# The small operations of the denominators on GpSimd, and attention a step farther behind the numerators

## The chip, the core and the metric

The kernel runs on one core of one Trainium2 chip. The metric is the device time of one execution in microseconds (us); lower is better. The core's engines run side by side, each works through its own queue of instructions in order, and they wait for one another by semaphores: TensorE (PE in the profile, with its weight loads as PEld), VectorE (DVE), ScalarE (ACT), GpSimd (POOL) and SyncE (SP), which here only issues DMA transfers.

## The reference

Everything is float32. With 2048 positions of 512 numbers, 32 heads of 16 numbers and a hidden size of 1792, it computes

```
g = sigmoid((x * gate_w).sum(-1))                      # one gate per position
q, k, v = split(x @ wqkv)                              # 32 heads x 16
phi(y)  = [softmax(y @ w_phi), softmax(-(y @ w_phi))]  # 32 features per head
kv      = sum over positions of phi(k)^T v             # per head 32 x 16
z       = sum over positions of phi(k)                 # per head 32
o       = (phi(q) @ kv) / (phi(q) . z + 1e-6)          # numerator / denominator
a       = o @ wo
b       = relu(x @ w1 + b1)^2 @ w2 + b2
out     = g * a + (1 - g) * b
```

## The kernel before

Float32 products are made from two rounded halves, a high one (h) and a low one (l), and three passes: high times high, low times high, high times low (`mm3`). A tile name that ends in h or l is such a half. The halves of a tile are made by a copy on ScalarE and a subtraction on VectorE or GpSimd (`split`).

The first 273 us make the hidden layer of the dense branch, the features of the keys with the sums kv and z, and the queries. None of that is touched by the change, and nothing more is said of it. The rest is a second stage of 56 **steps**, 14 for each of four blocks of 512 positions. A step multiplies one 128-wide slice of the hidden layer by one slice of w2 (`down`): four groups, for the 128-row parts of the block, into the four PSUM banks uA, uE, uB0 and uB1, three matmuls of 512 columns each. The hidden slices come back from HBM into tiles O0h/O0l (even steps) and O1h/O1l (odd steps), some as finished halves, some through a tile named ring that is split on the way. A slice is loaded or split up to four steps before its step.

Between the steps stand, for each block i:

- `do_e(i, k)`, for the four quarters k of the heads: load the queries, the exponentials, their sums sm and the reciprocals r = 1/sm.
- `do_phi(i, k)`: the denominators, and the features of the queries scaled by them. GpSimd multiplies the exponentials by z into ez (two halves of 128x512; there is one ez tile, so the next quarter waits until it is read); VectorE sums ez into dz (128x64); then come the **small operations**: dz times r; den, the sum of the two softmax parts of dz plus 1e-6; its reciprocal; and w = r times the reciprocal. VectorE scales the exponentials by w (128x1024) and transposes them (128x1024) into a tile that TensorE reads. For block 0 these tiles are the four named XA, for the other blocks the halves of tb (quarters 0 and 1) and phiT (quarters 2 and 3).
- `do_n(i)`: the **numerators**, one burst of 32 small matmuls (32x32 by 512) into the four PSUM banks vB, vE, kv, vA. It takes the quarters in the order 0, 2, 1, 3; quarter 3 is its last fourth. Then `split` reads the four banks into XS10h to XS21l.
- `attend(i, c)`, for c = 0 to 3: 12 matmuls of the numerators with wo into one of the same four banks, and one operation on VectorE that adds the result, times the gate, to the output row.
- `evict` at the end of a block's 14 steps: ScalarE copies a bank of `down` into XA times 1-g, and a **row addition** (128x512) adds that to the output row, on VectorE or GpSimd.

**What sets the order.** Nothing is issued as the code runs through. Each call of an engine is recorded in a plan. `Plan.order` (line 238) then goes through the plan with costs per instruction (`lengths`), due times counted back from TensorE's work, and one lock for VectorE and GpSimd operations with two wide inputs (`op.two`), and it writes one queue per engine. What is recorded on `nc.either` goes to VectorE or GpSimd, whichever the plan would start first. TensorE's groups keep the recorded order, but the plan may bring forward a group out of the first five (`LOOK`) if the groups ahead of it are not ready in its reckoning. On the chip every queue is in order, and an instruction whose input is late holds up what stands behind it.

The steps at which bursts and attention are recorded come from a table and a loop near the end (`steps`):

```
NUM = [13, 26, 38, 50]
when(NUM[i], do_n, i)
for c in range(NC):
    when(NUM[i] + 2 + c, attend, i, c)
```

Of the kernel before, what the change touches and what calls it, by code (L numbers as in the profile page):

```python
# [11 lines left out]
ALU = mybir.AluOpType  # L12
# [5 lines left out]
P = 128  # L18
S, D, H, DH, F = 2048, 512, 32, 16, 1792
# [16 lines left out]
CALM, LATE = 16.0, 2.0  # L36
PARTED = 8
FOLD = 8
NUM = [13, 26, 38, 50]
AT = [0, 1, 2, 4, 8, 11, 14, 17, 20, 23, 26, 29, 32, 35, 38, 41]  # L40


# [333 lines left out]
def tile_gated_mix(ctx: ExitStack, tc: tile.TileContext, xT, xn, wqT, wkT, wphi, wv, wo, w1, b1, w2, b2, gw, out):  # L376
    nc = Plan(tc.nc)
# [7 lines left out]
    def buf(tag, n=512, bufs=1, dtype=F32):  # L385

        i = turns[tag] = turns.get(tag, -1) + 1
        return View(Buffer(sbuf, shadows[n], f"{tag}_{i % bufs}", n, dtype), shadows[n])
# [298 lines left out]
    def scaled(e3, w):  # L687
        nc.vector.tensor_tensor(e3, e3, w.unsqueeze(2).to_broadcast([P, 2 * H, DH]), ALU.mult)
        return e3.rearrange("p h f -> p (h f)")
# [114 lines left out]
    def do_phi(i, k):  # L804
        e3, r = st["e", i, k]
        ez = buf("ez", 2 * D)
        by_rows = lambda t: t.rearrange("p (n f) -> p n f", f=4 * DH)
        e = by_rows(e3.rearrange("p h f -> p (h f)"))
        for half in range(2):
            s = slice(half * NG, (half + 1) * NG)  # L810
            z = zb[:, k * 4 * DH:(k + 1) * 4 * DH].unsqueeze(1).to_broadcast([P, NG, 4 * DH])
            nc.gpsimd.tensor_tensor(by_rows(ez)[:, s, :], e[:, s, :], z, ALU.mult)
        dz, w = small("dz", 2 * H, 2), small("w", 2 * H, 1)
        nc.vector.tensor_reduce(dz, ez.rearrange("p (h f) -> p h f", f=DH), AX.X, ALU.add)
        nc.either.tensor_tensor(dz, dz, r, ALU.mult)
        pair = lambda t: t.rearrange("p (h t) -> p h t", t=2)
        den = pair(dz)[:, :, 0]
        nc.vector.scalar_tensor_tensor(den, den, 1e-6, pair(dz)[:, :, 1], ALU.add, ALU.add)
        nc.vector.reciprocal(den, den)
        nc.either.tensor_tensor(pair(w), pair(r), den.unsqueeze(2).to_broadcast([P, H, 2]), ALU.mult)  # L820
        phi = scaled(e3, w)
        if i == 0:
            pt = buf(E_PLACES[k], 2 * D)
        else:
            if k % 2 == 0:
                st["pt"] = buf(("tb", "phiT")[k // 2], 4 * D)
            pt = st["pt"][:, k % 2 * 2 * D:(k % 2 + 1) * 2 * D]
        st["pt", i, k] = pt
        nc.vector.transpose(pt, phi)
# [173 lines left out]
    when = lambda s, f, *a: steps.setdefault(s, []).append(lambda: f(*a))  # L1003
# [3 lines left out]
    for i in range(NB):  # L1007
        when(AT[4 * i], gates, ORDER_B[i])
        for k in range(NK):
            if i:  # L1010
                when(max(AT[4 * i + k], NUM[0] if i == 1 else 0), do_e, i, k)
            when(max(AT[4 * i + k] + 2, NUM[i - 1] if i else 0), do_phi, i, k)
        when(NUM[i], do_n, i)
        for c in range(NC):
            when(NUM[i] + 2 + c, attend, i, c)
    for t in range(NT):
        for f in steps.get(t, ()):
            f()
        i, f = divmod(t, NF)
# [80 lines left out]
```

## Time and profile before

| | us |
|---|---|
| three runs | 484.23, 484.39, 485.07 (median 484.39) |
| the profiled execution, its time | 484.48 |
| its span, first to last instruction | 482.7 |
| TensorE busy | 477.8 (99%) |
| VectorE busy | 398.2 (82%) |
| ScalarE busy | 247.5 (51%) |
| GpSimd busy | 188.0 (39%) |

A row of a group gives engine, operation, output <- inputs, partitions x elements, the count, the busy time in us and the mean ns of one. A row of the timeline gives the start in us from the start of the span, the duration in us, the engine, the operation, and in brackets the idle time before it with what ended it. All of the work has source line 363, a helper that issues the plan, so tiles tell the rows apart. Tile names in the order of a queue carry the number of the operation that made them; the profile leaves these numbers out.

### The profile page before, as it was taken

What the parts mean: (1) busy time and instruction counts of PE and PEld (TensorE: products, weight loads), DVE (VectorE), ACT (ScalarE), POOL (GpSimd) and SP (SyncE); (2) the same over time, 40 slices, a digit from 0 to 9 for tenths busy, and PEclk for the clock granted to TensorE, in tenths of its full rate; (3) what the DMA queues carried; (4) which work ended last, traced back from release to release, by engine and by line L of the source; (5) the groups of instructions that cost most, each with busy time, mean ns of one, the idle gap of its engine ahead of it and who ended that gap; (6) DMA issues with size and microseconds to landing.
All of it is one profiled execution on the core that took longest, in us unless ns stands there. A gap on an engine that the chain in (4) does not pass through costs nothing.

```text
span 482.7 us, 9482 instructions
## 1 busy us (share of the span) xinstructions
PE 477.8 (99%) x3513; PEld 383.7 (79%) x3513; DVE 398.2 (82%) x565; ACT 247.5 (51%) x440; POOL 188.0 (39%) x160
## 2 busy tenths in 40 slices
PE   9999999999999999999999999999999999999997
PEld 4877788888888888888888888778878887888786
DVE  3997799988898757999888838999999999896214
ACT  5897879642698666426688803442245304420400
POOL 1010545743563202121022328667577808950000
PEclk9999999999999999999999999999999999999999
DMA  7999876885587779954799887824632572225302
GB/s 272 380 396 325 285 270 252 262 309 185 178 281 252 264 265 317 292 197 165 240 335 353 304 293 271 270 96 172 221 109 67 162 252 88 65 89 209 119 0 87
DMA packets 61654, 107.98 MB, mean 224 GB/s; under 512 B 6952, under 2 KB 11432, under 8 KB 61608
## 3 DMA queue, kind: packets, MB, share of 16 engines
q1 hardware_dynamic: 60768, 106.33, 64.0%
q10 hardware_dynamic: 808, 1.05, 0.9%
q8 instruction: 27, 0.44, 0.4%
q14 instruction: 19, 0.16, 0.1%
q0 software_dynamic: 32, 0.01, 0.0%
HBM read 62.27 MB, written 45.09 MB: 222 GB/s over the span
## 4 chain that ended last, share of the span: by engine, by line
PE 98%; DVE 1%; issue 0%
PE uB L363 30%; PE uA L363 18%; PE uE L363 17%; PE vB L363 11%; PE vE L363 8%; PE vA L363 8%; PE kv L363 5%; DVE tb L363 0%; DVE vE L363 0%; DVE uE L363 0%; DVE KT10l L363 0%; DVE KT10h L363 0%; DVE XS40l L363 0%; DVE XS30l L363 0%; DVE KT31l L363 0%; DVE O1l L363 0%
## 5 line engine op out<-in xcount | busy, mean ns | idle before, releaser
L363 POOL TENSOR_TENSOR ez<-XA,vext 128x512 f32<-128x512 f32 x24 | 34.9, 1469 | 13.7 <-ACT XA L363 6.5
L363 PE MATMUL uA<-XA,O0h 128*128 128x512 f32 x128 | 39.7, 391 | 0.0
L363 ACT ACTIVATE XA<-XA 128x512 f32<-128x512 f32 x24 | 13.9, 627 | 40.3 <-DVE XA L363 40.3
L363 ACT ACTIVATE row<-row 128x512 f32<-128x512 f32 x56 | 34.0, 623 | 0.3
L363 POOL TENSOR_TENSOR row<-row,wo 128x512 fp32r<-128x512 f32 x8 | 10.4, 1299 | 50.3 <-ACT wo L363 40.6
L363 PEld LDWEIGHTS uA<-XA,O0h 128*128 128x128 f32 x128 | 23.9, 188 | 5.1 <-ACT row L363 0.2
L363 PE MATMUL uA<-XA,O0l 128*128 128x512 f32 x64 | 24.9, 389 | 0.0
L363 POOL TENSOR_TENSOR row<-row,b2b 128x512 fp32r<-128x512 f32 x9 | 13.0, 1449 | 23.6 <-ACT b2b L363 16.3
L363 ACT ACTIVATE O0h<-ring 128x512 fp32r<-128x512 f32 x17 | 10.7, 628 | 21.0 <-PE uB L363 10.1
L363 DVE TENSOR_REDUCE dz<-ez 128x64 f32<-128x1024 f32 x16 | 19.3, 1209 | 1.8 <-POOL ez L363 1.2
L363 PE MATMUL uB<-XA,O3h 128*128 128x512 f32 x64 | 19.8, 391 | 0.0
L363 POOL TENSOR_TENSOR row<-row,XA 128x512 f32<-128x512 f32 x12 | 18.5, 1556 | 2.3 <-ACT row L363 1.3
L363 DVE SCALAR_TENSOR_TENSOR xn<-xn,gwb 128x512 f32<-128x512 f32 x16 | 11.3, 709 | 7.8 <-DMA xn<-in_xn 7.8
L363 DVE RECIPROCAL r<-sm 128x64 f32<-128x64 f32 x32 | 17.2, 539 | 0.3
L363 ACT ACTIVATE O1h<-ring 128x512 fp32r<-128x512 f32 x17 | 10.7, 627 | 13.0 <-PE uB L363 12.5
L363 DVE TENSOR_TENSOR XA<-XA,w 128x1024 f32<-128x1024 f32 x12 | 17.0, 1414 | 0.0
L363 ACT ACTIVATE wo<-row 128x512 fp32r<-128x512 f32 x17 | 10.7, 627 | 12.3 <-DMA hkept<-wo 10.2
L363 DVE TENSOR_REDUCE sm<-e 128x64 f32<-128x1024 f32 x11 | 13.4, 1216 | 3.6 <-ACT e L363 3.5
L363 ACT ACTIVATE row<-b2b,rest 128x512 f32<-128x512 f32 x16 | 10.8, 715 | 9.5 <-DMA out<-row 5.9
L363 POOL TENSOR_TENSOR O0l<-ring,O0h 128x512 fp32r<-128x512 f32 x9 | 14.2, 1582 | 3.5 <-ACT O0h L363 2.6
L363 DVE TENSOR_TENSOR e<-e,r 128x1024 f32<-128x1024 f32 x11 | 15.1, 1370 | 0.2
L363 POOL TENSOR_TENSOR O1l<-ring,O1h 128x512 fp32r<-128x512 f32 x9 | 13.1, 1460 | 5.3 <-ACT O1h L363 5.3
(936 smaller groups left out, 1742.4 us busy)
## 6 DMA issues: line engine op xcount, KB each, us to landing
hkept<-row SPq DMA_DIRECT2D x56, 256.0 KB, 4.2
ring<-hkept SPq DMA_DIRECT2D x24, 256.0 KB, 2.7
hkept<-b2b SPq DMA_DIRECT2D x16, 256.0 KB, 3.2
hkept<-wo SPq DMA_DIRECT2D x16, 256.0 KB, 4.1
xn<-in_xn SPq DMA_DIRECT2D x16, 256.0 KB, 4.8
O0h<-hkept SPq DMA_DIRECT2D x16, 256.0 KB, 3.2
O0l<-hkept SPq DMA_DIRECT2D x16, 256.0 KB, 3.4
O1h<-hkept SPq DMA_DIRECT2D x16, 256.0 KB, 3.7
```

Of the source, the lines that this page charges most:

```text
L363: call(*map(real, op.args), **{k: real(a) for k, a in op.kw.items()})
```

## The change

Three of the small operations are now bound to GpSimd. The operation on VectorE that added the two parts and 1e-6 in one instruction is two: the addition on GpSimd, and the addition of the constant on VectorE. The reciprocal stays on VectorE. The burst of numerators is recorded a step earlier for blocks 0 and 1. Attention is recorded three steps behind it instead of two for the blocks 0 to 2, so that it stays where it was for blocks 0 and 1 and is a step later for block 2. The loops that record `do_e` and `do_phi` of a block start no earlier than the burst of the block before, so the first of them for blocks 1 and 2 move forward by the same step in the record.

```
-NUM = [13, 26, 38, 50]
+NUM = [12, 25, 38, 50]
...
         dz, w = small("dz", 2 * H, 2), small("w", 2 * H, 1)
         nc.vector.tensor_reduce(dz, ez.rearrange("p (h f) -> p h f", f=DH), AX.X, ALU.add)
-        nc.either.tensor_tensor(dz, dz, r, ALU.mult)
+        nc.gpsimd.tensor_tensor(dz, dz, r, ALU.mult)
         pair = lambda t: t.rearrange("p (h t) -> p h t", t=2)
         den = pair(dz)[:, :, 0]
-        nc.vector.scalar_tensor_tensor(den, den, 1e-6, pair(dz)[:, :, 1], ALU.add, ALU.add)
+        nc.gpsimd.tensor_tensor(den, den, pair(dz)[:, :, 1], ALU.add)
+        nc.vector.tensor_scalar(den, den, 1e-6, None, ALU.add)
         nc.vector.reciprocal(den, den)
-        nc.either.tensor_tensor(pair(w), pair(r), den.unsqueeze(2).to_broadcast([P, H, 2]), ALU.mult)
+        nc.gpsimd.tensor_tensor(pair(w), pair(r), den.unsqueeze(2).to_broadcast([P, H, 2]), ALU.mult)
...
         when(NUM[i], do_n, i)
         for c in range(NC):
-            when(NUM[i] + 2 + c, attend, i, c)
+            when(NUM[i] + (3 if i < 3 else 2) + c, attend, i, c)
```

The plan then writes other queues from about 270 us of the span on. TensorE has the same matmuls. The first burst moves three matmuls back (behind the group of bank uB1 of its step), the second one whole step forward, the third and fourth keep their step; the attention of blocks 1 and 3 keeps its step, that of block 2 is one step later. VectorE has five rows fewer. Of the twelve row additions of blocks 0 to 2, four move from GpSimd to VectorE, two each of blocks 1 and 2.

**GpSimd ahead of the first burst.** w is the factor of one quarter, row a finished output row of block 0, ez the product with z. In the queue before:

```order
L363 TENSOR_TENSOR ez_3699<-phiT_2654,vext_97 128x512 x2
L363 TENSOR_TENSOR w_3737<-r_0_2819,dz_3675 128x64
L363 TENSOR_TENSOR O1l_3742<-ring_3624,O1h_3686 128x512
L363 TENSOR_TENSOR O2h_3765<-row_3543,Vt_0_3609 128x512
L363 TENSOR_TENSOR row_3768<-row_3768,XA_0_3774 128x512
L363 TENSOR_TENSOR row_3804<-row_3804,XA_0_3774 128x512
```

And in the queue of the change:

```order
L363 TENSOR_TENSOR ez_3699<-phiT_2654,vext_97 128x512 x2
L363 TENSOR_TENSOR w_3730<-r_0_2727,dz_3601 128x64
L363 TENSOR_TENSOR dz_3672<-dz_3672,r_0_2819 128x64
L363 TENSOR_TENSOR dz_3672<-dz_3672 128x32
L363 TENSOR_TENSOR dz_3737<-dz_3737,r_0_2837 128x64
L363 TENSOR_TENSOR dz_3737<-dz_3737 128x32
L363 TENSOR_TENSOR w_3785<-r_0_2819,dz_3672 128x64
L363 TENSOR_TENSOR row_3746<-row_3746,XA_0_3789 128x512
L363 TENSOR_TENSOR w_3817<-r_0_2837,dz_3737 128x64
L363 TENSOR_TENSOR row_3754<-row_3754,XA_0_3789 128x512
```

The small operations of the last two quarters have come in, and the factor w of the last quarter now stands between two row additions; the low half O1l and the half O2h have gone to VectorE.

**VectorE ahead of the first burst.** phiT holds the exponentials of quarters 2 and 3, the transposes write the XA that the burst reads. Before:

```order
L363 TENSOR_REDUCE dz_3739<-ez_3699 128x64
L363 TENSOR_TENSOR phiT_2654<-phiT_2654,w_3737 128x1024
L363 TENSOR_TENSOR dz_3739<-dz_3739,r_0_2837 128x64
L363 STREAM_TRANSPOSE XA_0_3763<-phiT_2654 128x1024
L363 SCALAR_TENSOR_TENSOR dz_3739<-dz_3739 128x32
L363 RECIPROCAL dz_3739<-dz_3739 128x32
L363 TENSOR_TENSOR w_3795<-r_0_2837,dz_3739 128x64
L363 TENSOR_TENSOR phiT_2654<-phiT_2654,w_3795 128x1024
L363 STREAM_TRANSPOSE XA_0_3813<-phiT_2654 128x1024
```

Now:

```order
L363 TENSOR_TENSOR O1l_3719<-ring_3631,O1h_3688 128x512
L363 SCALAR_TENSOR_TENSOR xn_3635,lg_3723<-xn_3635,gwb 128x512
L363 TENSOR_REDUCE dz_3737<-ez_3699 128x64
L363 TENSOR_TENSOR tb_2484<-tb_2484,w_3730 128x1024
L363 TENSOR_SCALAR dz_3672<-dz_3672 128x32
L363 STREAM_TRANSPOSE XA_0_3766<-tb_2484 128x1024
L363 RECIPROCAL dz_3672<-dz_3672 128x32
L363 TENSOR_SCALAR dz_3737<-dz_3737 128x32
L363 RECIPROCAL dz_3737<-dz_3737 128x32
L363 TENSOR_TENSOR phiT_2654<-phiT_2654,w_3785 128x1024
L363 STREAM_TRANSPOSE XA_0_3805<-phiT_2654 128x1024
L363 TENSOR_TENSOR phiT_2654<-phiT_2654,w_3817 128x1024
```

The two-input small operations have left the queue, a half (O1l) and an operation of the gates (xn) have come in, and the last two scalings take their factors from GpSimd.

**VectorE ahead of the second burst.** XS30h and XS30l are queries of block 2, XA exponentials, phiT the tile that the second burst reads last. Before:

```order
L363 STREAM_TRANSPOSE phiT_4155<-XA_0_3936 128x1024
L363 SCALAR_TENSOR_TENSOR dz_4095<-dz_4095 128x32
L363 TENSOR_REDUCE ends_4166<-XS30l_4072 128x32
L363 RECIPROCAL dz_4095<-dz_4095 128x32
L363 TENSOR_TENSOR XA_0_4174<-XS30h_4048,ends_4133 128x1024
L363 TENSOR_REDUCE ends_4166<-XS30l_4072 128x32
L363 TENSOR_REDUCE ends_4190<-XS31h_4105 128x32 x2
L363 TENSOR_REDUCE sm_4205<-XA_0_4174 128x64
L363 RECIPROCAL r_4215<-sm_4205 128x64
L363 TENSOR_TENSOR XA_0_4008<-XA_0_4008,w_4183 128x1024
L363 STREAM_TRANSPOSE phiT_4155<-XA_0_4008 128x1024
```

Now:

```order
L363 STREAM_TRANSPOSE phiT_4167<-XA_0_3947 128x1024
L363 TENSOR_TENSOR XA_0_3995<-XA_0_3995,w_4161 128x1024
L363 TENSOR_REDUCE ends_4184<-XS30l_4074 128x32
L363 STREAM_TRANSPOSE phiT_4167<-XA_0_3995 128x1024
L363 TENSOR_TENSOR XA_0_4199<-XS30h_4048,ends_4138 128x1024
```

The work for block 2 that stood ahead of the last scaling and transpose of block 1 stands behind them.

## The prediction

> **What bounds the kernel now.** I read the page first, for the shares of the engines and the chain of waits.
>
> ```profile
> span 482.7 us, 9482 instructions
> PE 477.8 (99%) x3513; PEld 383.7 (79%) x3513; DVE 398.2 (82%) x565; ACT 247.5 (51%) x440; POOL 188.0 (39%) x160
> PEclk9999999999999999999999999999999999999999
> PE 98%; DVE 1%; issue 0%
> ```
>
> TensorE is busy all but 4.9 us of the span, 98% of the chain that ended last is TensorE, and the granted clock is full in every slice. The change adds and removes no matmul. It can therefore only move the time by TensorE's waits, and a share of 99% cannot say whether any wait is left in the part that is changed. For that I read TensorE's timeline around the four bursts of numerators: the last matmul of `down` ahead of each, the first one behind it, and the weight loads in between.
>
> ```profile
> 313.02 0.39 PE L363 MATMUL uB<-KB110h,O0l 128*128 128x512 f32 x1
> 314.83 0.10 PEld L363 LDWEIGHTS vB<-XA,kvb 32*32 32x32 f32 x1 [0.18 <-DVE XA L363]
> 315.85 0.50 PE L363 MATMUL uB<-KB110h,O0h 128*128 128x512 f32 x1
> ...
> 357.24 0.39 PE L363 MATMUL uB<-KB221h,O1l 128*128 128x512 f32 x1
> 357.56 0.10 PEld L363 LDWEIGHTS vB<-tb,kvb 32*32 32x32 f32 x1 [0.35 <-issue]
> 358.75 0.10 PEld L363 LDWEIGHTS vB<-phiT,kvb 32*32 32x32 f32 x1
> 359.84 0.50 PE L363 MATMUL uA<-KT40h,O0h 128*128 128x512 f32 x1
> ...
> 403.26 0.39 PE L363 MATMUL uB<-KT31h,O1l 128*128 128x512 f32 x1
> 405.86 0.50 PE L363 MATMUL uA<-KB220h,O0h 128*128 128x512 f32 x1
> ...
> 449.28 0.39 PE L363 MATMUL uB<-KB211h,O1l 128*128 128x512 f32 x1
> 451.88 0.50 PE L363 MATMUL uA<-KT30h,O0h 128*128 128x512 f32 x1
> ```
>
> From matmul to matmul the bursts take 2.60 us (359.84 - 357.24, 405.86 - 403.26, 451.88 - 449.28), and the first one takes 2.83 (315.85 - 313.02). So the first burst waits **0.23 us**, for an XA of VectorE, and the others wait for nothing. All that waits in the changed part is 0.23 us; that is the most that this change can win. A burst wants its quarter 3 at 358.75 - 357.56 = 1.19 us after its first load.
>
> How near the others are to a wait is read from VectorE, whose last transpose of each block feeds the burst:
>
> ```profile
> 293.00:315.00 22.00, 22.00 (x147) 17.40 (x153) 21.52 (x27) 8.60 (x14) 16.30 (x14) 1.00 0.74 245
> 315.00:358.00 43.00, 43.00 (x230) 34.51 (x217) 42.43 (x55) 13.96 (x24) 29.84 (x25) 1.00 0.47 153
> ...
> 312.27 1.23 DVE L363 TENSOR_TENSOR phiT<-phiT,w 128x1024 f32<-128x1024 f32 x1
> 313.53 1.25 DVE L363 STREAM_TRANSPOSE XA<-phiT 128x1024 f32<-128x1024 f32 x1
> ...
> 350.46 1.16 DVE L363 TENSOR_TENSOR XA<-XS30h,ends 128x1024 f32<-128x1024 f32 x1
> 355.03 1.61 DVE L363 TENSOR_TENSOR XA<-XA,w 128x1024 f32<-128x1024 f32 x1
> 356.67 1.25 DVE L363 STREAM_TRANSPOSE phiT<-XA 128x1024 f32<-128x1024 f32 x1
> ...
> 395.12 1.24 DVE L363 STREAM_TRANSPOSE phiT<-XA 128x1024 f32<-128x1024 f32 x1
> 439.90 1.25 DVE L363 STREAM_TRANSPOSE phiT<-XA 128x1024 f32<-128x1024 f32 x1
> ```
>
> In the two rows of windows (columns: sum of the stretch, then busy us of PE, PEld, DVE, ACT, POOL) VectorE is busy 21.52 of 22 and 42.43 of 43 us: up to the second burst it is as full as TensorE. The transposes end 0.8 us before quarter 3 is wanted in the second burst (357.92 against 358.75), and about 7 and 8 us before the third and fourth burst begin (396.4 and 441.2). So the change is decided at the first two bursts.
>
> **The change part by part.** The small operations, as groups of the part behind 257 us, with single rows below:
>
> ```profile
> L363 DVE SCALAR_TENSOR_TENSOR dz<-dz 128x32 f32<-128x32 f32 x16 | 7.4, 468 | 0.0
> L363 DVE TENSOR_TENSOR w<-r,dz 128x64 f32<-128x64 f32 x8 | 3.8, 474 | 0.1
> L363 DVE TENSOR_TENSOR dz<-dz,r 128x64 f32<-128x64 f32 x3 | 1.8, 600 | 0.0
> L363 DVE TENSOR_SCALAR ge<-ge 128x4 f32<-128x4 f32 x2 | 0.3, 170 | 0.5 <-ACT ge L363 0.5
> L363 DVE TENSOR_TENSOR O1l<-ring,O1h 128x512 fp32r<-128x512 f32 x4 | 5.5, 1379 | 2.3 <-ACT O1h L363 2.3
> L363 DVE TENSOR_TENSOR XS10l<-vB,XS10h 128x512 fp32r<-128x512 f32 x4 | 2.7, 680 | 6.8 <-ACT XS10h L363 6.8
> L363 DVE TENSOR_REDUCE dz<-ez 128x64 f32<-128x1024 f32 x16 | 19.3, 1209 | 1.8 <-POOL ez L363 1.2 <-POOL w L363 0.4
> L363 DVE RECIPROCAL dz<-dz 128x32 f32<-128x32 f32 x16 | 5.2, 331 | 0.0
> ...
> 372.42 2.99 POOL L363 TENSOR_TENSOR ez<-XA,vext 128x512 f32<-128x512 f32 x2
> 374.19 1.28 DVE L363 SCALAR_TENSOR_TENSOR dz<-dz 128x32 f32<-128x32 f32 x1
> 306.31 0.33 POOL L363 TENSOR_TENSOR w<-r,dz 128x64 f32<-128x64 f32 x1 [1.69 <-DVE dz L363]
> 310.14 1.39 POOL L363 TENSOR_TENSOR row<-row,XA 128x512 f32<-128x512 f32 x1 [0.99 <-ACT XA L363]
> 309.37 0.69 ACT L363 ACTIVATE XA<-uA,rest 128x512 f32<-128x512 f32 x1 [4.75 <-PE uA L363]
> ```
>
> A 128x32 operation with two inputs took 1.28 us on VectorE while GpSimd ran ez, and ended (375.47) just behind it (375.41): with two inputs in SBUF each, one of the two engines stands until the other is done. All such small operations took 7.4 + 3.8 + 1.8 = 13.0 us of VectorE. The change takes them off and leaves 16 additions of a constant, 0.17 us each by the only row of that kind, 2.7 us. VectorE is relieved of about 10 us over the stage; it takes over four row additions, 0.68 us free (the XS10l row) to 1.4 us against GpSimd (the O1l row) each. GpSimd's 0.33 us for each small operation falls into a share of 39%.
>
> *First burst.* TensorE reaches it three matmuls later, 0.68 us, so quarter 3 is wanted at 313.02 + 0.32 (from the last matmul to the first load, 357.56 - 357.24) + 0.68 + 1.19 = 315.2. (Without the 0.68 it is 314.5; the transpose ended at 314.78, which agrees with the 0.23.) VectorE's queue from 293.3 to there: by the starts in the timeline, a reduction that is done earlier now (1.1), three additions of dz (0.9), two products with r (1.4) and two factors w (1.1) leave, 4.5 us; three subtractions of halves (0.68 to 1.4 each), one xn (0.7) and three additions of a constant (0.5) come in, 3.2 to 5.4. The last transpose, which ended at 314.78, ends between 313.5 and 315.7. GpSimd gives a second bound: the last factor w stands behind the first row addition, which waits for ScalarE's copy of uA, which TensorE times, and so starts at 310.14 as now. 310.14 + 1.39 + 0.33 = 311.9; VectorE's scaling and transpose then take 312.27 to 314.78, 2.5 us: 314.4, or 315.7 if the next row addition gets in first (1.3). The wait is thus between 0 and 0.5 us where it was 0.23. Two of the four ends lie before 315.2 and two half a microsecond behind it. I take 0.13, nearer to the early ends, because the late ones need a blocked operation each: **-0.1 us**, between -0.23 and +0.3.
>
> *Second burst.* TensorE reaches it one step (12 matmuls, 2.72 us) and 0.23 us earlier: quarter 3 is wanted at 358.75 - 2.95 = 355.8. VectorE needed 43.1 us from the one last transpose to the other (314.78 to 357.92). The operations for block 2 from 350.46 to 355.03, 4.6 us, now stand behind, and an xn (0.7) is done earlier: 37.8 us. From 313.5 to 315.7 this gives 351.3 to 353.5, at least 2.3 us early: **0 us**. If that cover goes, the burst waits by what is missing.
>
> *Third and fourth burst.* Two row additions each come in, at most 2 x 1.4 us against some 7 us of slack: 0. *Attention.* For block 0 it stays 12 matmuls behind the burst, for block 2 it gets a step more room; it had no wait: 0. *SP's queue.* Block 2's output rows leave a step later, and the loads behind them are for the step at about 444 us (two steps before 449.5). The loads were issued at 437.81 and land in 3 us:
>
> ```profile
> 437.81 0.38 SPq L363 DMA_DIRECT2D O0h<-hkept  x1
> O0h<-hkept SPq DMA_DIRECT2D x16, 256.0 KB, 3.2
> ```
>
> The last row operation of block 2 moves from 433.3 to about 436, the load to 438 at most, and it lands 3 us early: 0.
>
> The sum is 484.48 - 0.1 = 484.4 against the profiled execution. Its 484.48 stand 0.09 above the median of the runs, 484.39, so on the scale of the runs I expect **484.3 us**.
>
> **The rivals.** *The last quarter is late (slower).* If VectorE is at its late bound, its scaling of quarter 2 comes at about 310.8 and meets the row addition that started at 310.14: it stands until 311.5, the scaling of quarter 3 starts at 313.9 and can meet the next row addition, 1.3 more. With 2.5 us for it and its transpose the end is 316.4 to 317.7, the wait 1.2 to 2.5 us, the change +1.0 to +2.3: 485.4 to 486.7, say 486.0. It decides from a transpose later than 316.4 on. For it: the order of GpSimd, where w stands between two rows. Against: both collisions are needed, and VectorE's early end is as likely as its late one. *The additions of a constant stand like the operations they replace (slower).* If one of them beside a running GpSimd takes 1.28 us as the old operation did, and not 0.17, the three ahead of the first burst make its last transpose up to 3.3 us later, 316.8 to 319.0, and the wait 1.6 to 3.8: 485.8 to 488.0. For it: the new operation has its input and output in SBUF too. Against: it has one input, and the reductions and reciprocals, with one input each, kept their times beside GpSimd (means of 1209 and 331 ns in the groups above). All three would have to be hit; no row here has an addition of a constant beside a running GpSimd. The Trainium skill bears on this: "SBUF — State Buffer", section "SBUF: two separate sides", says that VectorE and GpSimd share one pair of ports as an exclusive lock, and that a VectorE operation in a two-port mode takes it as well as one with two inputs; "VectorE: DVE Perf Modes", section "Mode 2×_2P — use both read ports for one tensor", counts a float32 addition of a constant in SBUF among that mode's operations. The row at 374.19 agrees with the lock; nothing here shows the mode. *The second burst comes too early (slower).* It was brought forward 2.72 us and had 0.8. If GpSimd's factors hold VectorE up by 4 us in the 38, for instance because its rows stand behind VectorE's two-input operations, it waits 1 to 2 us: 485.9. Against: GpSimd is busy 29.84 of 43 us there and gets only four additions, 1.3 us. *A real gain (faster).* More than 0.97 us would have to be found; only 0.23 us of waits stand in the rows, and the tail behind the last matmul is not touched. It would need matmuls to follow faster than now. About 483.3. *The change does not act on the time at all*, because the small operations never held TensorE: 484.4, which the forecast cannot be told from.
>
> **How the numbers follow.** What can be told from no change is 0.2%, 0.97 us: 483.4 to 485.4. The forecast with its neighbours up to +0.9 us (the ends of the first burst, and no effect) has 0.85; its own range is 484.0 to 485.0. The late last quarter has 0.05, the additions of a constant that stand 0.03, the early second burst 0.04, the real gain 0.03. Faster 0.03, same 0.85, slower 0.12. The range runs from 483.9 (all of the 0.23 us won, and the runs' scatter below the median) to 485.3.
>
> **What would show it.** First burst: 2.60 us between its neighbours and no load that names an XA of VectorE, or at most 2.9. Second burst: 2.60, and its last transpose at least 2 us ahead. VectorE's busy time should fall from 398.2 by 4 to 8 us with the time unchanged. Additions of a constant of more than 0.3 us beside a running GpSimd would speak for the second rival. The prediction is wrong if TensorE's busy share falls or a load in a burst waits for a microsecond.

## The result, and the profile after

| | before | after |
|---|---|---|
| median of the runs, us | 484.39 (483.74 to 488.92, 11 runs) | 488.59 (485.47 to 489.38, 11 runs) |
| ratio | | 1.0061, 95% interval 1.0036 to 1.0085 |
| the profiled execution, its time | 484.48 | 488.59 |
| its span | 482.7 | 486.8 |

The change makes the kernel slower, by 0.4 to 0.9% by the interval. The ratio of the medians, 1.0087, is larger, since the runs of the change spread from 485.5 to 489.4 us. Five of the eleven runs of the change, and 23 of the 89 runs of the kernel before that were taken beside the experiments, had a mean granted clock of 0.992 to 0.997 and took 487 to 492 us, which makes the intervals below wide; the median of the others is 486.9 and 484.2 us, and the text goes by the medians of all runs and by traces. The first lines of the page of the changed kernel:

```profile
span 486.8 us, 9481 instructions
PE 479.8 (99%) x3513; PEld 383.8 (79%) x3513; DVE 399.7 (82%) x559; ACT 246.7 (51%) x440; POOL 192.3 (40%) x182
PEclk9999999999999999999999999989999999999999
PE 86%; DVE 8%; DMA 4%; issue 0%; SPq 0%; ACT 0%; DVEq 0%
```

TensorE's share is still 99%, and VectorE's busy time has not fallen (399.7 against 398.2). What has changed is the chain: of TensorE's 98% there, 12 points have gone to VectorE and to transfers, and in one slice the granted clock is not full. TensorE's timeline at the first two bursts says where:

```profile
313.56 0.39 PE L363 MATMUL uB<-KB110h,O0l 128*128 128x512 f32 x1
313.88 0.10 PEld L363 LDWEIGHTS vB<-XA,kvb 32*32 32x32 f32 x1 [0.35 <-issue]
315.48 0.10 PEld L363 LDWEIGHTS vB<-XA,kvb 32*32 32x32 f32 x1 [1.42 <-DVE XA L363]
318.19 0.12 PEld L363 LDWEIGHTS vB<-XA,kvb 32*32 32x32 f32 x1 [2.46 <-DVE XA L363]
318.19 1.06 PE L363 MATMUL vB<-XA,kvb 32*32 32x512 f32 x1 [1.56 <-DVE XA L363]
320.08 0.79 PE L363 MATMUL uA<-KB111h,O1h 128*128 128x512 f32 x1
321.46 0.40 PE L363 MATMUL uE<-KB111h,O1h 128*128 128x512 f32 x1
...
358.65 0.39 PE L363 MATMUL uB<-KB220h,O0l 128*128 128x512 f32 x1
361.25 0.50 PE L363 MATMUL uA<-KB221h,O1h 128*128 128x512 f32 x1
362.05 0.40 PE L363 MATMUL uE<-KB221h,O1h 128*128 128x512 f32 x1
```

The second burst takes 2.60 us between its neighbours, as before, and so do the third and the fourth. The first takes 6.52 (320.08 - 313.56) where it took 2.83. Two of its loads wait for an XA of VectorE, that of quarter 2 and that of quarter 3. Quarter 3 was wanted at 313.88 + 1.19 = 315.07 and came at 318.19: 3.12 us late. The rest is the clock. From 316 us on, the windows of 2 us (their sum, the busy us of PE, PEld, DVE, ACT, POOL, then the granted clock, the share of the transfers and their GB/s):

```profile
316.00:318.00 2.00, 0.63 (x32) 0.00 (x0) 1.97 (x2) 0.00 (x0) 2.00 (x2) 0.99 0.65 248
318.00:320.00 2.00, 1.81 (x16) 0.23 (x16) 2.00 (x2) 0.00 (x0) 1.20 (x1) 0.50 0.04 8
320.00:322.00 2.00, 2.00 (x14) 1.59 (x7) 1.45 (x3) 1.80 (x4) 0.00 (x0) 0.66 0.00 0
```

TensorE has 0.63 us of work from 316 to 318, and then runs at half its clock until past 320. The last loads to the next matmul of `down` take 1.89 us (320.08 - 318.19) against 1.02 before (315.85 - 314.83), 0.87 more, and the first three matmuls of `down` take 1.38 (321.46 - 320.08) against 0.80 behind the second burst (362.05 - 361.25), some 0.6 more. Before, quarter 3 was 0.30 late by the same reckoning (314.83 - 313.34 - 1.19). 3.12 + 0.87 + 0.6 - 0.30 is 4.3; the burst begins 0.14 earlier than the three matmuls ahead of it explain (313.56 against 313.02 + 0.68). That leaves 4.1 to 4.2, the 4.1 us of the span.

**Why VectorE was late.** Groups of VectorE from 286 us to the end of block 0's last transpose, before (to 315 us):

```profile
L363 DVE SCALAR_TENSOR_TENSOR dz<-dz 128x32 f32<-128x32 f32 x4 | 2.2, 545 | 0.0
L363 DVE TENSOR_TENSOR dz<-dz,r 128x64 f32<-128x64 f32 x3 | 1.8, 600 | 0.0
L363 DVE TENSOR_TENSOR w<-r,dz 128x64 f32<-128x64 f32 x2 | 1.2, 588 | 0.1
L363 DVE TENSOR_TENSOR XS41l<-row,XS41h 128x512 fp32r<-128x512 f32 x1 | 0.7, 679 | 0.0
L363 DVE TENSOR_TENSOR phiT<-phiT,w 128x1024 f32<-128x1024 f32 x2 | 3.1, 1544 | 0.0
```

and after (to 319 us):

```profile
L363 DVE TENSOR_SCALAR dz<-dz 128x32 f32<-128x32 f32 x4 | 2.4, 601 | 0.0
L363 DVE TENSOR_TENSOR O1l<-ring,O1h 128x512 fp32r<-128x512 f32 x2 | 2.3, 1145 | 0.0
L363 DVE TENSOR_TENSOR O2h<-row,Vt 128x512 fp32r<-128x512 f32 x1 | 1.8, 1777 | 0.0
L363 DVE TENSOR_TENSOR XS41l<-row,XS41h 128x512 fp32r<-128x512 f32 x1 | 1.8, 1771 | 1.4 <-ACT XS41h L363 1.4
L363 DVE TENSOR_TENSOR phiT<-phiT,w 128x1024 f32<-128x1024 f32 x2 | 3.8, 1898 | 0.0
```

5.2 us of small operations have left VectorE here. The additions of a constant that came in took 2.4 us, not 0.7 (four of 0.17). The two O1l and the O2h are new, 4.1 us. XS41l, the same operation as before, took 1.77 instead of 0.68, and the two scalings 3.8 instead of 3.1. The sum dz of the first quarter starts at 287.54 and at 287.58, the last transpose ends at 314.78 and at 318.14: **VectorE's path** from the one to the other has grown from 27.24 to 30.56 us.

The price of the constant is best seen beside GpSimd's rows. The group over the stage, then single rows of both engines:

```profile
L363 DVE TENSOR_SCALAR dz<-dz 128x32 f32<-128x32 f32 x16 | 8.8, 551 | 0.0
...
302.38 3.47 POOL L363 TENSOR_TENSOR ez<-phiT,vext 128x512 f32<-128x512 f32 x2 [2.30 <-DVE dz L363]
304.64 1.25 DVE L363 TENSOR_SCALAR dz<-dz 128x32 f32<-128x32 f32 x1
308.76 1.24 POOL L363 TENSOR_TENSOR dz<-dz,r 128x64 f32<-128x64 f32 x1 [0.71 <-DVE dz L363]
309.74 0.30 DVE L363 TENSOR_SCALAR dz<-dz 128x32 f32<-128x32 f32 x1
311.35 0.11 DVE L363 TENSOR_SCALAR dz<-dz 128x32 f32<-128x32 f32 x1
348.73 1.30 POOL L363 TENSOR_TENSOR O0l<-ring,O0h 128x512 fp32r<-128x512 f32 x1 [0.23 <-ACT O0h L363]
348.87 1.20 DVE L363 TENSOR_SCALAR dz<-dz 128x32 f32<-128x32 f32 x1
```

The three that overlap a running GpSimd operation end at 305.89, 310.04 and 350.07; GpSimd's end at 305.85, 310.00 and 350.03. So each stands until GpSimd is done, and 0.04 us more. With GpSimd idle it took 0.11. The mean, 551 ns, is above the 468 ns of the operation that it replaced, and the sixteen took 8.8 us, where the prediction had 2.7: VectorE's relief over the stage was not about 10 us but 13.0 - 8.8, some 4, which other work filled.

Last, the work of the two late quarters, GpSimd's rows and VectorE's:

```profile
311.50 0.32 POOL L363 TENSOR_TENSOR w<-r,dz 128x64 f32<-128x64 f32 x1 [1.18 <-DVE dz L363]
311.78 1.28 POOL L363 TENSOR_TENSOR row<-row,XA 128x512 f32<-128x512 f32 x1
314.23 0.32 POOL L363 TENSOR_TENSOR w<-r,dz 128x64 f32<-128x64 f32 x1 [1.16 <-DVE phiT L363]
314.50 4.70 POOL L363 TENSOR_TENSOR row<-row,XA 128x512 f32<-128x512 f32 x3
...
311.86 2.29 DVE L363 TENSOR_TENSOR phiT<-phiT,w 128x1024 f32<-128x1024 f32 x1
315.35 1.50 DVE L363 TENSOR_TENSOR phiT<-phiT,w 128x1024 f32<-128x1024 f32 x1
316.89 1.25 DVE L363 STREAM_TRANSPOSE XA<-phiT 128x1024 f32<-128x1024 f32 x1
```

The first scaling meets the row addition and takes 2.29 us instead of some 1.23. The w of quarter 3, behind that row on GpSimd, then stands until the scaling is done (314.15): there is one tile w in the kernel (`small("w", 2 * H, 1)`), and the scaling reads it. GpSimd's next rows start behind it, at 314.50, and the second scaling meets them (1.50).

### The profile page after: what moved, and what is told of

Same layout as the page of the kernel before. It is cut to its first block, busy times and chain, and to the rows that moved or that the text cites. A ratio compares the mean times of both kernels' runs of the same rounds, so it can differ in the third digit from the quotient of the medians.

```text
span 486.8 us, 9481 instructions
## 1 busy us (share of the span) xinstructions
PE 479.8 (99%) x3513; PEld 383.8 (79%) x3513; DVE 399.7 (82%) x559; ACT 246.7 (51%) x440; POOL 192.3 (40%) x182
## 3 DMA queue, kind: packets, MB, share of 16 engines
q10 hardware_dynamic: 808, 1.05, 0.7%
## 4 chain that ended last, share of the span: by engine, by line
PE 86%; DVE 8%; DMA 4%; issue 0%; SPq 0%; ACT 0%; DVEq 0%
PE uB L363 26%; PE uE L363 15%; PE uA L363 15%; PE vB L363 10%; PE vE L363 8%; PE vA L363 7%; PE kv L363 4%; DVE dz L363 1%; DMA KT11l<-in_xT 1%; DMA wkept<-O0l 1%; DMA row<-in_wo 1%; DMA tb<-in_xT 1%; DVE XA L363 1%; DVE phiT L363 1%; DVE tb L363 1%; DVE O1l L363 1%
## 5 line engine op out<-in xcount | busy, mean ns | idle before, releaser
L363 POOL TENSOR_TENSOR ez<-XA,vext 128x512 f32<-128x512 f32 x24 | 40.7, 1714 | 18.6 <-DVE ends L363 7.0
L363 DVE TENSOR_REDUCE dz<-ez 128x64 f32<-128x1024 f32 x16 | 19.3, 1204 | 4.7 <-POOL ez L363 4.5
L363 DVE SCALAR_TENSOR_TENSOR xn<-xn,gwb 128x512 f32<-128x512 f32 x16 | 13.5, 843 | 4.5 <-DMA xn<-in_xn 4.5
L363 DVE TENSOR_TENSOR XS10l<-vB,XS10h 128x512 fp32r<-128x512 f32 x4 | 2.7, 682 | 16.3 <-ACT XS10h L363 16.3
L363 DVE TENSOR_TENSOR XA<-XA,w 128x1024 f32<-128x1024 f32 x12 | 15.3, 1278 | 0.0
L363 ACT ACTIVATE e<-e 128x512 f32<-128x512 f32 x22 | 13.0, 623 | 3.9 <-DVE e L363 3.7
L363 DVE TENSOR_REDUCE sm<-XA 128x64 f32<-128x1024 f32 x12 | 14.2, 1202 | 0.0
```

What stands on the lines that cost most here:

```text
L363: call(*map(real, op.args), **{k: real(a) for k, a in op.kw.items()})
```

## The experiments

Diffs are against the changed kernel; where the text starts from the kernel before, it says so. "..." stands for lines left out, which in the runs that move or leave out an operation give it a name (`op.tag`) to be found by. The first four take the change apart. Theory A blames the small operations, theory B the shifted steps.

**Small operations alone:** `NUM` and the steps of attention as before, the rest of the change kept.

```
-NUM = [12, 25, 38, 50]
+NUM = [13, 26, 38, 50]
...
-            when(NUM[i] + (3 if i < 3 else 2) + c, attend, i, c)
+            when(NUM[i] + 2 + c, attend, i, c)
```

> The small operations go to GpSimd as in the change; numerators and attention keep the steps that they had. Theory A (the small operations make the late quarters of block 0, by their hand-overs between GpSimd and VectorE): TensorE still waits 1.5 to 3.2 us between the quarters of the first burst, the neighbours of that burst stand 4.1 to 6.6 us apart against 2.83 before, and the time is 486 to 489. Theory B (the shifted steps make it): the burst takes 2.6 to 2.9 us and the time is 484.0 to 484.8.

485.54 us (485.1 to 486.03), ratio 1.0004 [0.9973, 1.0035]. The neighbours of the first burst stand 3.25 us apart, with a wait of 0.60. Neither figure of the expectation: it is 1.2 us slower than before by the median, far less than the change. VectorE is not earlier here: its last transpose of block 0 ends at 318.83, against 318.14 in the change. But the plan put the first burst a whole step later (behind 12 more matmuls than in the change), so that quarter 3 is wanted at 318.16 and not at 315.07, which hides most of it.

**Steps alone:** the small operations as before, the rest of the change kept.

```
-        nc.gpsimd.tensor_tensor(dz, dz, r, ALU.mult)
+        nc.either.tensor_tensor(dz, dz, r, ALU.mult)
...
-        nc.gpsimd.tensor_tensor(den, den, pair(dz)[:, :, 1], ALU.add)
-        nc.vector.tensor_scalar(den, den, 1e-6, None, ALU.add)
+        nc.vector.scalar_tensor_tensor(den, den, 1e-6, pair(dz)[:, :, 1], ALU.add, ALU.add)
...
-        nc.gpsimd.tensor_tensor(pair(w), pair(r), den.unsqueeze(2).to_broadcast([P, H, 2]), ALU.mult)
+        nc.either.tensor_tensor(pair(w), pair(r), den.unsqueeze(2).to_broadcast([P, H, 2]), ALU.mult)
```

> Only the steps are shifted (numerators one step earlier for two blocks, attention a step farther behind for three); the small operations stay where they were. Theory A: the first burst is as before, 2.6 to 2.9 us between its neighbours, the time 484.0 to 484.8, with at most the 0.23 us of the old wait to gain. Theory B: a wait of 1.5 to 3.2 us stands in the first burst, 486 to 489.

489.34 us, ratio 1.0077 [1.0034, 1.0119]: theory B's side, and slower than the change itself (the waits of the first burst are 1.40 and 3.62 us). But TensorE reaches the burst with the same matmuls ahead of it as before. It is again VectorE that is late, by another set of collisions. VectorE's and GpSimd's rows:

```profile
310.84 5.98 POOL L363 TENSOR_TENSOR row<-row,XA 128x512 f32<-128x512 f32 x4 [0.73 <-ACT XA L363]
313.14 1.27 DVE L363 SCALAR_TENSOR_TENSOR dz<-dz 128x32 f32<-128x32 f32 x1
315.83 1.07 DVE L363 TENSOR_TENSOR w<-r,dz 128x64 f32<-128x64 f32 x1
319.49 0.10 PEld L363 LDWEIGHTS vB<-XA,kvb 32*32 32x32 f32 x1 [3.62 <-DVE XA L363]
```

Here the old small operations stand beside the row additions: 1.27 and 1.07 us, where they took 0.14 and 0.23 in the kernel before (at 311.44 and 312.01, as one row of GpSimd ended, at 311.53, and before the next, which waited for ScalarE until 312.79). The step in the record changes due times; the plan gives the queues another order; and the order decides what meets what.

**The w ahead of the row:** the changed kernel with two instructions of GpSimd exchanged in the finished order.

```
-        for op in self.order():
+        ops = self.order()
+        at = {op.tag: j for j, op in enumerate(ops) if op.tag}
+        first = min((j for t, j in at.items() if t[0] == "row"))
+        row, last = ops[first], ops[at["w", 0, 3]]
+        ops.remove(row)
+        ops.insert(ops.index(last) + 1, row)
+        for op in ops:
...
```

> The changed kernel with two instructions of GpSimd in another order: the first addition of a finished row of block 0 is issued behind the w of the last quarter instead of ahead of it. If the w that stood behind that row is what makes the last quarter late (first rival of the prediction), the row's 1.28 us and the collision with phiT times w (2.29 us against some 1.0 to 1.5) leave the path: the last wait of the burst falls from 2.46 us to 0 to 1.2, the time to 485.3 to 487.2. If the additions of the constant beside GpSimd make it (second rival), the waits of the burst stay within 0.5 us of the 1.42 and 2.46 us that the change had, and the time at 488 to 489.

486.13 us (485.32 to 486.41), within the first rival's 485.3 to 487.2. The waits are 0.36 and 1.96 us, so quarter 2 comes 1.4 us sooner and the neighbours stand 4.60 apart; the first scaling takes 1.22 us instead of 2.29:

```profile
311.49 1.22 DVE L370 TENSOR_TENSOR phiT<-phiT,w 128x1024 f32<-128x1024 f32 x1
316.77 0.10 PEld L370 LDWEIGHTS vB<-XA,kvb 32*32 32x32 f32 x1 [1.96 <-DVE XA L370]
```

The last wait was expected to fall to at most 1.2 and stayed at 1.96: with this collision gone, VectorE's queue itself is still late. Quarter 3 is late by 2.08 us (316.77 - 313.50 - 1.19) instead of 3.12. So the collision accounts for 1.0 us; the rest of the gain by the median (2.5) is about what the clock had cost, which stays at 1.00 in this trace.

**Without the additions of the constant:**

```
-        for op in self.order():
+        for op in [o for o in self.order() if not o.tag or o.tag[0] != "eps"]:
...
+        nc.ops[-1].tag = ("eps", i, k)
...
```

> The changed kernel without its 16 additions of 1e-6 on VectorE: the constant in the denominator is left out, nothing else. If these additions make the quarters late (second rival: 1.25, 0.30 and 0.11 us ahead of the first burst), the waits of the burst fall by 1.4 to 1.8 us together and the time to 486 to 487. If the place of w decides (first rival), VectorE only waits for GpSimd instead, the waits fall by less than 0.5 us, and the time stays at 488 to 489.

484.93 us (484.63 to 486.92), ratio 0.9994 [0.9956, 1.0031], below both ranges of the expectation. One wait is left:

```profile
315.67 0.10 PEld L364 LDWEIGHTS vB<-XA,kvb 32*32 32x32 f32 x1 [0.51 <-DVE XA L364]
```

The neighbours stand 3.16 us apart instead of 6.52. The waits fell by 3.4 us, twice what the second rival had expected and more than the 2.4 us that the four additions took: O0l fell from 1.45 to 0.97, XS41l from 1.77 to 0.96. Quarter 3 is late by 0.63 us (315.67 - 313.85 - 1.19), and the clock stays at 1.00. And it shows that even without them the change wins nothing.

The next four ask what the additions' price is made of, what the clock adds, and which step it is.

**The additions of the constant on GpSimd:** the whole computation, nothing else moved.

```
         for op in self.order():
+            if op.tag and op.tag[0] == "eps":
+                op.engine = "gpsimd"
...
```

> The changed kernel with its 16 additions of 1e-6 issued on GpSimd, right behind the addition of the pair, and nothing else moved: the whole computation. If these additions cost VectorE their 0.11 to 1.25 us because they wait for GpSimd's work and push the other operations against it (what leaving them out suggests: 4.2 us of waits in the first burst became 0.5), the first burst needs 3.0 to 4.0 us between the weight loads around it against 6.74 in the change and 3.05 before, and the time is 484.4 to 485.8. If it is the number of hand-overs and GpSimd's longer queue, a further operation of 0.24 to 0.32 us there in each denominator makes it no better: 487 to 489.

489.59 us, ratio 1.0099 [1.0067, 1.0131]: the second answer, and 0.6 above its bound. VectorE is relieved of 8 us over the kernel (391.7 busy instead of 399.7), and the first burst takes 7.82 us between its neighbours. Rows of the denominator of quarter 1:

```profile
305.93 0.29 POOL L366 TENSOR_SCALAR dz<-dz 128x32 f32<-128x32 f32 x1
306.25 0.35 DVE L366 RECIPROCAL dz<-dz 128x32 f32<-128x32 f32 x1 [0.29 <-POOL dz L366]
306.30 1.29 POOL L366 TENSOR_TENSOR ez<-phiT,vext 128x512 f32<-128x512 f32 x1
306.52 1.61 DVE L366 TENSOR_TENSOR O1l<-ring,O1h 128x512 fp32r<-128x512 f32 x1
```

VectorE now waits for GpSimd's 0.29 us, and the O1l behind it, 0.63 us in the change, meets the ez that the old place had let pass. My reading of the run without the additions was too simple: taking the operation away frees both engines; moving it only hands the collision on to the next operation with two inputs. What the trace shows is no gain, not a loss: VectorE's path takes 30.73 us (288.63 to 319.36) against 30.56 in the change. It starts 1.05 later, because GpSimd's first ez of the block starts at 286.05 instead of 285.01; z comes for it from HBM, by transfers issued from 279.4 to 280.7 us that took 5.2 to 5.8 us to land, instead of 3.6 to 3.8. They stand ahead of all that was edited; whether the median's 1.0 us come from them was not tried.

**Filled idle time:** 14 matmuls of no use ahead of the first burst.

```
         for op in self.order():
+            if op.tag == ("n", 0) and not done:
+                done = True
+                self.filler()
...
+    def filler():
+        one = lambda n: nc.const_aps.tensor(1.0, (P, n), mybir.dt.bfloat16)
+        for _ in range(14):
+            tc.nc.tensor.matmul(banks["vB"], one(P), one(512), start=True, stop=True, skip_group_check=True)
...
```

> The changed kernel with 14 matmuls of no use (some 3.2 us) put on TensorE right ahead of the first burst; the work of all other engines stands in the same order. They stand in the idle time, so that TensorE never idles for more than about 0.5 us. If the granted clock of 0.50 and 0.66 behind the burst came from TensorE's idle time, the clock stays at 1.00 from 312 to 326 us and the time falls by 0.6 to 2.0 us against the changed kernel, to 486.5 to 488. If the clock fell for another reason, it falls here too and the time is that of the change or up to 1 us above.

487.40 us, span 484.9 instead of 486.8, within the first answer's range. The windows behind the filling:

```profile
316.00:318.00 2.00, 2.00 (x54) 0.86 (x65) 1.96 (x3) 0.00 (x0) 2.00 (x2) 1.00 0.23 88
318.00:320.00 2.00, 2.00 (x36) 1.05 (x6) 2.00 (x2) 1.16 (x3) 0.74 (x1) 1.00 0.03 8
```

With more work on TensorE, the same queues elsewhere and the burst wanting its quarters later, the clock stays at 1.00 and the kernel is 1.9 us shorter in the trace, 1.2 by the median; the mean clock of all ten runs is 0.999 or 1.000. So the half clock came from TensorE's idle time.

**Numerators alone:** the kernel before with `NUM = [12, 25, 38, 50]`.

> The kernel before with the numerators of blocks 0 and 1 a step earlier, attention as it was. In the order the burst stands half a step later than before, and VectorE gets the tensors of quarter 1 behind the sum of quarter 3, as in the run of both steps. If the earlier step alone makes VectorE's queue late, the first burst waits 2 to 4 us and the time is 486 to 490; if the step of attention made it, the burst takes 2.6 to 3.0 us and the time is 484.0 to 484.8.

486.05 us (484.14 to 488.0), ratio 1.0023 [0.9995, 1.0051]. The profiled execution has a wait of 0.34 us and 2.99 between the neighbours, which is the second answer, but the median lies in the first answer's range, 1.6 us above the kernel before, and the runs spread over 3.9 us. Why they spread isn't settled.

**Both causes removed:** the constant on GpSimd, and the w ahead of the row.

> The changed kernel with the additions of 1e-6 on GpSimd and the first addition of a finished row behind the w of the last quarter. If both causes are there and add up, nothing waits in the first burst: 2.6 us between its neighbours, 484.0 to 484.4, at or 0.2 us under the kernel before. If only one of them holds the burst at a time, it comes out as with the additions on GpSimd alone, within 0.3 us.

487.17 us, ratio 1.0042 [1.0011, 1.0072], 4.92 between the neighbours: neither answer. Against the constant on GpSimd alone it wins the 2.4 us that the exchange of w and row wins in the changed kernel (488.59 to 486.13); the constant on GpSimd costs 1.0 by the medians here too (486.13 to 487.17). Again VectorE's path in the trace is no longer for it (29.53 us, 288.07 to 317.60, against 29.63 with the exchange alone, 287.09 to 316.72), and GpSimd's first ez starts 0.98 later (285.50 against 284.52).

The last four complete the table of the three edits and test the plan.

**Attention alone:** the kernel before with attention a step farther behind.

> The kernel before with attention a step farther behind the numerators for three blocks, the numerators where they were. In the order the first burst stands half a step (six matmuls, 1.4 us) earlier than before, and VectorE's queue ahead of its last quarter holds one subtraction of a half more (O1l). If the lateness of VectorE's queue for its burst is all that counts, this is a wait of 1 to 3 us and 485.0 to 487.5; with the numerators alone at 486.05 and both steps at 489.34 the two would then about add up. If attention's step does nothing by itself, 484.0 to 484.8.

492.54 us (four runs), ratio 1.0136 [1.0058, 1.0214], the slowest of all, where 487.5 was the upper bound. The burst is reached 1.1 us earlier than before and quarter 3 waits 5.19 us:

```profile
310.30 2.11 POOL L363 TENSOR_TENSOR row<-row,XA 128x512 f32<-128x512 f32 x1
311.19 1.31 DVE L363 TENSOR_TENSOR dz<-dz,r 128x64 f32<-128x64 f32 x1
315.62 2.18 DVE L363 TENSOR_TENSOR phiT<-phiT,w 128x1024 f32<-128x1024 f32 x1
319.14 0.10 PEld L363 LDWEIGHTS vB<-XA,kvb 32*32 32x32 f32 x1 [5.19 <-DVE XA L363]
```

The product with r, 0.21 us before, took 1.31 and the last scaling 2.18 instead of 1.23.

**Small operations and attention; small operations and numerators:** the changed kernel with `NUM` as before, and the changed kernel with attention as before.

> The changed kernel with the numerators of blocks 0 and 1 back at their old steps: small operations on GpSimd and attention a step farther behind. In the order the first burst stands nine matmuls (2.0 us) later than in the change, the queue of VectorE ahead of it holds the same kinds of work. If the burst was too early for the queue that the small operations leave, the 4.2 us of waits in the burst fall to 0 to 1.5 us, and the time to 484.4 to 486. If the queue itself grows with the delay, the wait stays over 2 us and the time is 486.5 to 489.

> The changed kernel with attention back at its old steps: small operations on GpSimd and the numerators a step earlier. The planner answers by putting the first burst 18 matmuls (4.1 us) later than in the change, and three additions of finished rows (some 1.0 us each) on VectorE ahead of the numerators of quarters 2 and 3. If only the balance of the two counts, 4.1 us less 3 us leaves 1 us less wait than in the change, 485.5 to 487.5. If the rows, now without GpSimd beside them, cost less, there is no wait and the time is 484.0 to 485.

The first: 485.35 us (485.02 to 486.18), one wait of 0.70, as its first answer. The second: 487.03 us, within the first answer, but not for its reason: the first burst takes 2.63 us and the second 3.52, so a wait of 0.9 us has moved to the second burst, where the prediction's third rival had looked for it; the other 1.8 us of the span are smaller waits elsewhere (0.42 and 0.32 ahead of 273 us, 0.41 for a transfer at 394.9). All eight combinations, with the median in us and the time between the neighbours of the first burst (before: 484.18 to 484.47 in the four series):

| | steps as before | numerators earlier | attention farther | both |
|---|---|---|---|---|
| small operations as before | 484.4; 2.83 | 486.05; 2.99 | 492.54; 8.86 | 489.34; 7.40 |
| small operations on GpSimd | 485.54; 3.25 | 487.03; 2.63 | 485.35; 3.35 | 488.59; 6.52 |

The effects do not add. With the small operations on GpSimd attention's step costs nothing by itself (485.54 and 485.35), and without them it costs 8 us.

**The plan knows the price:** the changed kernel, whose plan holds that an addition of a constant, too, cannot run beside GpSimd's operations on two tensors.

```
-        op.two = method in ("tensor_tensor", "scalar_tensor_tensor") and len(wide) > 1 and ...
+        op.two = method == "tensor_scalar" or method in ("tensor_tensor", "scalar_tensor_tensor") and len(wide) > 1 and ...
```

> The changed kernel, whose planner is told that an addition of a constant cannot run beside GpSimd's operations on two tensors, as it already holds of the operations on two tensors. In the order the first burst moves back by three matmuls (0.7 us), one half goes from VectorE to GpSimd and two go to VectorE behind the first transposes. If the price of these additions that the planner didn't know is what spoils its order, the burst needs 3.0 to 4.5 us between the weight loads around it (6.74 in the change) and the time is 484.4 to 486.5. If its other prices are as far off (subtractions of halves at 0.6 that take 1.45 to 1.78 us), the time stays at 486.5 to 489.

485.65 us (484.7 to 486.2), ratio 1.0000 [0.9966, 1.0035]; one wait of 1.20 us in the first burst, 4.07 us between the weight loads around it, and 0.61 us in the second: the first answer.

```profile
316.67 0.10 PEld L363 LDWEIGHTS vB<-XA,kvb 32*32 32x32 f32 x1 [1.20 <-DVE XA L363]
```

With the same operations in another order, some of them on the other engine of the two, 2.9 us of the 4.2 are back. The mean of the 16 additions falls from 551 to 402 ns, but the four ahead of the first burst still take 0.79, 1.26, 0.30 and 0.11 us, 2.5 together. The gain there is in the halves, which take 4.3 us instead of 7.3 in their new places; VectorE's path is 29.26 us (287.36 to 316.62). None of these kernels beats the one before, which has only 0.23 us of waits to give in the first burst.

## Why the prediction was wrong

*What bounds the kernel.* Right: TensorE's waits alone count. The 4.1 us are the waits of the first burst and what they did to the clock. That at most 0.23 us could be won held too: no kernel of the twelve was faster than the one before.

*Later bursts, attention, SP's queue at 0.* Right in the changed kernel: 2.60 us at the second to fourth burst. The small operations with the earlier numerators show that the second burst could wait (2.60 to 3.52, 0.92 us).

*First burst.* Here the forecast failed: the end of VectorE's last transpose was put too early, and with it the wait of the burst, 3.12 us where 0 to 0.5 was expected. The transpose was put between 313.5 and 315.7, and ended at 318.14, 2.4 us above the upper end. By its own terms:

- "three additions of a constant (0.5)" took 1.25 + 0.30 + 0.11 = 1.66 us: 1.2 too little. This is the term that was mis-sized most, and it stood on the row of a 128x4 operation without GpSimd beside it.
- The queue from 293.3 on was taken to start as before. It started at 294.06 instead of 293.31, 0.75 later, behind an addition of the constant of 0.74 us and an XS41l of 1.77 instead of 0.68. The sum began at 293.3 and left out what the change does ahead of it; the reduction of 1.1 us that it had as leaving stands there too.
- The two scalings were taken at the old 1.86 and 1.23 us, and took 2.29 and 1.50: 0.7.
- The three halves took 4.07 us, inside their bounds of 2.0 to 4.2 but at the top; the 4.5 us that leave agree.

0.75 + 1.2 + 0.7 is 2.65; with the halves 0.1 under their upper bound, that is the miss of 2.4 within 0.2.

*GpSimd's bound.* The first row addition was put at 310.14, since it waits for ScalarE. It started at 311.78, because the w ahead of it waited for VectorE's reciprocal until 311.50. The bound left out that GpSimd's queue is in order and now waits for VectorE in each quarter.

*The rivals.* The first (the w between two row additions, both collisions) and the second (the constant that stands) were both right and came together, which no case of mine held; I gave them 0.05 and 0.03. By the medians the exchange of w and row wins 2.5 us and leaving out the constants 3.7, out of 4.2. They overlap, because either keeps the clock at 1.00, and so wins its 1.4 us as well: the lateness of quarter 3 falls by 1.0 us (3.12 to 2.08) and by 2.5 (3.12 to 0.63). The second rival had the end of the transpose, 316.8 to 319.0, and the wait, 1.6 to 3.8, about right; its time, 485.8 to 488.0, was too low by the clock. Its working was only in part so: it had three additions that stand for 1.28 us each, and one of the three did (1.25); the rest was the fourth one, ahead of 293.3, and the halves and scalings. The argument against the second, that reductions and reciprocals with one input kept their times, does not carry over to the addition of a constant. The Trainium skill, "VectorE: DVE Perf Modes", section "Mode 2×_2P — use both read ports for one tensor", counts a float32 operation with a constant in SBUF among those that use both read ports. The Trainium skill, "SBUF — State Buffer", section "SBUF: two separate sides", says that such an operation and one of GpSimd exclude each other. The trace agrees: the additions ended 0.04 us behind GpSimd's operations, while the sums dz and the reciprocals kept their means (1204 and 329 ns after, 1209 and 331 before). I gave the pages' rule too small a chance because no row of the kernel before had the case; a rule that no row speaks against deserves more than that.

*The clock* was in no case of the prediction; it was put at nothing without a reason. It adds about 1.4 us in the profiled execution (0.8 to 0.9 in the burst's last loads and matmuls, 0.6 behind them).

*Moving work.* "Perfetto Trace Analysis" of the Trainium skill, section "Optimizing Scalar/DVE Operations", says that moving operations between VectorE and GpSimd might not help since they share a port. The runs agree: 8 us less busy time on VectorE, with the constants on GpSimd, left its path at 30.73 us against 30.56, and the kernel came out at 489.59.

## What to carry to other kernels

The time of an operation on VectorE with operands in SBUF is not its own: with two inputs, or as an addition of a constant, it lasted in these traces until GpSimd's running operation was done (0.11 us alone, 1.25 beside an ez). So the price of moving work between these two engines is the set of operations that meet, to be read from both timelines side by side; and a price that a row shows without GpSimd beside it is a lower end, not the value.

A queue that was 0.3 us late at a burst had no room for a new order at its old costs. Where a planner makes the order, every edit of a step makes another one: tell it the true price of each new operation before judging the edit.

## What the runs showed of the hardware

**TensorE's clock fell in a short pause.** In the changed kernel TensorE had 0.63 us of work from 316 to 318 us, its longest pause between matmuls being 1.56 us; the granted clock was 0.50 in the two microseconds behind it and 0.66 in the next two. It also fell to 0.50 in the three traces with longer pauses at the first burst: 1.82 us (the constants on GpSimd), 2.72 (the steps alone) and 4.29 (attention alone). It stayed at 1.00 where the longest pause was 1.05 us (the w ahead of the row) or 1.36 (both causes removed), and where the pause was filled. The Trainium skill, "TensorE: Matmul & The Clock Gate", section "What's actually happening", says that the clock halves after an idle window of about 3.4 us, that the window runs freely, and so from run to run differently. The half rate agrees; but the pause of 1.56 us is less than half that window. What has to be idle for the clock to fall, and why it fell in some runs only, of the kernel before too, was not tried.

**The wait for GpSimd is exact.** Of the additions of the constant shown above, each that overlapped GpSimd ended 0.04 us behind it, whether that was an ez, a half or a small product of 128x64.
